# Attention and feed-forward on one core: the first product of seven tiles as Strassen's seven block products

## The chip, the core and the metric

The kernel runs on one core of a Trainium2 chip. Time is device microseconds (us) of one execution; lower is better. The core has TensorE (PE in the profile, its weight loads PEld), VectorE (DVE), ScalarE (ACT), GpSimd (POOL) and SyncE (SP), which only issues DMAs here. Each engine works through its own list in order; semaphores tie the lists together. A matmul takes a stationary operand of 128 columns (loaded first, `lhsT`) and streams a moving operand past it into PSUM.

## The reference

```python
# q, k, v: (8, 8, 576, 64) float32; w_in (512, 2048), w_out (2048, 512)
q_s = exp(q - max(q, -1));  q_s /= sum(q_s, -1) + 1e-9       # softmax over a row of 64
k_s = exp(k - max(k, 2));   k_s /= sum(k_s, 2) + 1e-9        # softmax over the sequence
kv  = einsum('bhsd,bhse->bhde', k_s, v)
att = einsum('bhsd,bhde->bhse', q_s, kv)
x   = att.transpose(0, 2, 1, 3).reshape(4608, 512)
h   = maximum(x @ w_in, 0)
out = (h * h) @ w_out
```

Nearly all the arithmetic is in the two products with `w_in` and `w_out`, both with 4608 rows of x.

## The kernel before

**Tiles.** The 4608 rows are nine tiles t = 0 to 8 of M = 512 columns (x is held transposed, features on the partitions). Tiles 0 to 7 are the first 512 rows of each batch, tile 8 the 64 last rows of all eight. While the feed-forward part works on tile t, the attention part makes tile t + 1, in four steps p of two heads each.

**Precision.** Each operand of a large product is split in a high part, rounded to float32r, and a low part, the rest: `split_x` makes xh on ScalarE and xl on VectorE, the weights are split once (`split_words`) into wi_h, wi_l, wo_h, wo_l, which stay in SBUF. A product is three matmuls: high by high, high by low, low by high.

**One tile.** For f = 0 to 15 (128 columns of w_in each), `first` makes a block h of 128 by 512 in a PSUM bank: 4 blocks of 128 features, 3 matmuls each, 12 of 512 columns. ScalarE makes r = relu(h), VectorE h = max(h, 0) * r, ScalarE gh = r squared and VectorE gl = h - gh (`split_g`). `second` adds gh and gl by w_out into four PSUM banks acc_0 to acc_3, again 12 matmuls of 512 columns, two groups later (LA = 2). The last two groups of `second` and the stores stand at the tile's end.

**Attention beside it.** For batches from 2 on q lies in blocks of 32; the maxima and sums of two half rows are exchanged by four small DMAs each (`swap_halves`, tiles sw_m and sw_s). `blocks_exp`, `blocks_norm`, `blocks_turn`, `blocks_split` make ql and qh; `k_max`, `k_shift_pool`, `k_exp` the keys; `kv_product` and `x_product` are its matmuls. `step`, `step_between` and `step_after` place these parts among the groups f, so a tile of the loop is written out in one order, and each engine's list is that order. Only tile 0 and what is before it is ordered by a planner.

## Time and profile before

| | |
|---|---|
| median of 3 runs | 883.64 us (883.05 to 884.48) |
| span of the profiled execution | 881.9 us |
| busy, PE / DVE / ACT / POOL | 865.1 / 485.8 / 359.7 / 186.8 us |
| tile 2 (232.62 to 326.29) | 93.67 us, PE busy 93.67 |
| tile 7, with no attention beside it (702.92 to 789.96) | 87.04 us |
| granted clock of TensorE | 0.998 of full |

The span is counted from the first to the last instruction of one profiled execution; the median is of unprofiled runs and is 1.7 us more. A matmul's shown duration (0.39 us for 512 columns) is longer than the step from one to the next, since matmuls overlap; the step is what counts. In the views a row gives line, engine, operation, output and inputs, count, busy time and mean of one in ns, and then the idle time ahead of it and what ended it. Nearly all instructions carry one line number, that of the helper which records them, so rows are told apart by tile names.

### The profile page before, as it was taken

How to read it: one execution, taken by the hardware profiler on the slowest of the kernel's cores; microseconds unless marked ns; L12 is line 12 of the kernel's file. 1: busy time of each engine (PE TensorE's matmuls, PEld its weight loads, DVE VectorE, ACT ScalarE, POOL GpSimd, SP SyncE). 2: the span in 40 equal slices, each digit the busy share in tenths (PEclk: the TensorE clock that was granted, in tenths of full speed). 3: DMA queues.
4: the chain of work that ended last, by engine and by line, in shares of the span. 5: the costliest groups of instructions: out<-in, count | busy, mean ns of one | idle time of the engine just before them, and what ended most of it. 6: DMA issues, size and time to landing. Idle time of an engine off the chain costs nothing.

```text
span 881.9 us, 12457 instructions
## 1 busy us (share of the span) xinstructions
PE 865.1 (98%) x4456; PEld 714.6 (81%) x4456; DVE 485.8 (55%) x897; ACT 359.7 (41%) x668; POOL 186.8 (21%) x237
## 2 busy tenths in 40 slices
PE   7899999999999999999999999999999999999997
PEld 6678888888888888788888888888888888888886
DVE  6888976554655465545654565556564532233222
ACT  5878854333434342335333343334233422232221
POOL 5789982111111101110111112110111000000000
PEclk9999999999999999999999999999999999999999
DMA  9992122211311122112311222113111110010002
GB/s 262 376 349 70 37 50 73 53 29 37 85 39 39 39 63 80 39 38 57 86 39 39 46 72 48 30 38 93 39 38 39 54 50 1 0 48 1 1 1 48
DMA packets 140878, 57.89 MB, mean 66 GB/s; under 512 B 115600, under 2 KB 134032, under 8 KB 140688
## 3 DMA queue, kind: packets, MB, share of 16 engines
q1 hardware_dynamic: 139104, 55.79, 23.6%
q10 hardware_dynamic: 1712, 1.31, 0.5%
q8 instruction: 35, 0.57, 0.3%
q14 instruction: 27, 0.22, 0.1%
HBM read 46.14 MB, written 10.49 MB: 64 GB/s over the span
## 4 chain that ended last, share of the span: by engine, by line
PE 91%; DMA 3%; DVE 3%; issue 1%; ACT 1%; SPq 1%; POOL 0%; DVEq 0%; POOLq 0%; ACTq 0%
PE acc L100 43%; PE h L100 42%; PE x L100 3%; PE kv L100 2%; DMA q<-in_q_dram 1%; DMA raw<-in_moe_w_in_dram 1%; DMA sw_m<-bmx 1%; SPq L100 1%; DVE km L100 1%; DMA kt<-in_k_dram 0%; DVE w L100 0%; POOL w L100 0%; DVE gl L100 0%; DVE up L100 0%; DVE qt L100 0%
## 5 line engine op out<-in xcount | busy, mean ns | idle before, releaser
L100 PE MATMUL h<-xh,w 128*128 128x512 f32 x1152 | 379.3, 392 | 3.2 <-DVE gl L100 3.1
L100 PE MATMUL acc<-w,gh 128*128 128x512 f32 x1152 | 355.7, 390 | 0.0
L100 PEld LDWEIGHTS h<-xh,w 128*128 128x128 f32 x1152 | 216.2, 188 | 50.3 <-DVE gl L100 4.4
L100 PEld LDWEIGHTS acc<-w,gh 128*128 128x128 f32 x1152 | 214.7, 188 | 43.4
L100 PE MATMUL h<-xl,w 128*128 128x512 f32 x576 | 224.3, 389 | 0.0
L100 PE MATMUL acc<-w,gl 128*128 128x512 f32 x576 | 224.2, 389 | 0.0
L100 DVE SCALAR_TENSOR_TENSOR h<-h,r 128x512 f32<-128x512 f32 x144 | 99.4, 691 | 101.8 <-ACT r L100 101.0
L100 DVE TENSOR_TENSOR gl<-h,gh 128x512 fp32r<-128x512 f32 x144 | 99.2, 689 | 92.2 <-ACT gh L100 83.7
L100 ACT ACTIVATE r<-h 128x512 f32<-128x512 f32 x144 | 85.1, 591 | 152.2 <-PE h L100 151.8
L100 ACT ACTIVATE gh<-r 128x512 fp32r<-128x512 f32 x144 | 90.7, 630 | 122.2 <-PE acc L100 113.7
L100 PEld LDWEIGHTS acc<-w,gl 128*128 128x128 f32 x576 | 108.1, 188 | 22.8
L100 PEld LDWEIGHTS h<-xl,w 128*128 128x128 f32 x576 | 108.2, 188 | 21.3
L100 POOL TENSOR_TENSOR k<-k,kmx 128x512 f32<-128x512 f32 x24 | 30.8, 1282 | 171.9 <-issue 143.1
L100 POOL PARTITION_ALL_REDUCE kmx<-km x24 | 17.4, 724 | 207.4 <-DVE km L100 166.2
L100 ACT ACTIVATE q<-q 128x576 f32<-128x576 f32 (+1 forms) x32 | 21.5, 672 | 96.7 <-DVE q L100 87.9
L100 POOL TENSOR_TENSOR w<-w,raw 128x512 int32<-128x512 int32 x32 | 42.0, 1320 | 7.9 <-DVE w L100 2.8
L100 POOL TENSOR_TENSOR w<-w,w 128x512 fp32r<-128x512 f32 x32 | 41.1, 1299 | 5.8 <-ACT w L100 5.7
L100 DVE SCALAR_TENSOR_TENSOR bsm<-bsm,sw_s 128x18 f32<-128x18 f32 x24 | 5.6, 232 | 61.4 <-DMA sw_s<-bsm 61.4
L100 ACT ACTIVATE raw<-raw 128x1024 f32<-128x1024 f32 (+1 forms) x32 | 36.3, 1148 | 2.2 <-DMA raw<-in_moe_w_in_dram 2.0
L100 DVE TENSOR_TENSOR bmx<-bmx,sw_m 128x18 f32<-128x18 f32 x24 | 4.2, 176 | 53.0 <-DMA sw_m<-bmx 53.0
L100 ACT ACTIVATE kvh<-kv,ks 64x64 fp32r<-64x64 f32 x64 | 19.8, 309 | 29.4 <-DVE ks L100 28.9
L100 ACT CAST qh<-qT 128x576 fp32r<-128x576 f32 (+1 forms) x32 | 20.9, 653 | 26.2 <-DVE qT L100 24.6
(104 smaller groups left out, 666.8 us busy)
## 6 DMA issues: line engine op xcount, KB each, us to landing
k<-in_k_dram SPq DMA_DIRECT2D x32, 256.0 KB, 2.7
raw<-in_moe_w_in_dram SPq DMA_DIRECT2D x16, 512.0 KB, 8.5
raw<-in_moe_w_out_dram SPq DMA_DIRECT2D x16, 512.0 KB, 8.8
out_dram<-o SPq DMA_DIRECT2D x32, 256.0 KB, 2.4
v<-in_v_dram SPq DMA_DIRECT2D x56, 128.0 KB, 2.9
q<-in_q_dram SPq DMA_DIRECT2D x96, 72.0 KB, 2.4
sw_m<-bmx SPq DMA_DIRECT2D x96, 2.2 KB, 1.7
sw_s<-bsm SPq DMA_DIRECT2D x96, 2.2 KB, 1.7
```

Of the source, the lines that this page charges most:

```text
L100: getattr(self.eng, op)(*map(real, args), **{k: real(a) for k, a in kwargs.items()})
```

## The change

Tiles 2 to 8 of the loop make the first product differently. Take two neighbouring groups of w_in columns, one = 2i and two = 2i + 1: 512 features by 256 columns, as 2 by 2 blocks of 256 by 128 (a11, a12 of group one, a21, a22 of group two), and x's tile as blocks b11, b12, b21, b22 of 256 features by 256 rows. Strassen's scheme in Winograd's form makes the four result blocks from seven block products instead of eight, with sums of blocks:

- of weights: s1 = a21 + a22, s2 = s1 - a11, s3 = a11 - a21, s4 = a12 - s2;
- of x: t1 = b12 - b11, t2 = b22 - t1, t3 = t2 - b11, t4 = b21 - t2.

Each of the seven operand pairs is again split in high and low, so a product is 2 x 3 matmuls of 256 columns (`product`). a11 b11, s2 t2, s3 t3 and a22 t4 add up one after the other in the left half of one PSUM bank (hu); ScalarE copies the running sum out after each (u1, u2, u3, c2's left half). s1 t1 and later s4 b22 add up in the right half of the other bank (hv), a12 b21 stands in its left. VectorE adds the pieces into c1 and c2 in SBUF and makes max(c, 0) * c; the high part is a copy on ScalarE, the low part of c2 is VectorE's, that of c1 GpSimd's.

The weights' sums don't fit in SBUF. In tile 1 they are made on GpSimd (`add_sums`), split (`split_sums`) and written to a DRAM buffer w_sums by ScalarE's queue (`keep_sums`), one of eight pairs at each of eight groups f; a11, a12 and a22 go there by SyncE (`begin_sums`). From tile 2 on, ScalarE's queue loads the pieces of pair n + 2 back into two rings of four former w_in slabs (`load_sums`), 1.8 MB per pair. The former slabs 2, 3 and 8 to 11 hold the split x parts. Tile 1's last two groups of `second` are carried over into tile 2; from then on `second` runs in eight units per pair, placed between the block products of the next pair, and the attention parts run two groups earlier (SKEW = 2), by new step functions.

On TensorE a pair of groups of tile 4 read like this before (group f = 5, the end of its first product and the start of a second):

```order
L100 MATMUL h_5_4501<-xh_2_4248,w_845 128x512
L100 MATMUL h_5_4501<-xh_3_4252,w_845 128x512
L100 MATMUL h_5_4501<-xl_3_4254,w_845 128x512
L100 MATMUL h_5_4501<-xh_3_4252,w_845 128x512
L100 MATMUL acc_0_4389<-w_845,gh_3_4441 128x512 x2
L100 MATMUL acc_0_4389<-w_845,gl_3_4443 128x512
L100 MATMUL acc_1_4393<-w_845,gh_3_4441 128x512 x2
L100 MATMUL acc_1_4393<-w_845,gl_3_4443 128x512
```

and now (pair f = 2, 3 of tile 5; h_3 is hu, h_2 is hv, each x6 row is one block product, the w names are slabs):

```order
L1138 MATMUL h_3_6122<-w_625,w_1342 128x256 x6
L1138 MATMUL h_2_6131<-w_709,w_1342 128x256 x6
L100 MATMUL acc_0_6138<-w_709,gh_1_6086 128x512 x2
L100 MATMUL acc_0_6138<-w_709,gl_1_6088 128x512
L1138 MATMUL h_3_6122<-w_1074,w_1420 128x256 x6
L1138 MATMUL h_2_6131<-w_1156,w_1420 128x256 x6
L100 MATMUL acc_1_6168<-w_709,gh_1_6086 128x512 x2
L100 MATMUL acc_1_6168<-w_709,gl_1_6088 128x512
L100 MATMUL acc_2_6172<-w_709,gh_1_6086 128x512 x2
L100 MATMUL acc_2_6172<-w_709,gl_1_6088 128x512
L1138 MATMUL h_3_6122<-w_1222,w_1486 128x256 x6
```

The second product, which stood in one piece of 12 matmuls behind a group, now stands in units of three between products that add into one PSUM block.

On ScalarE the end of a tile read like this before (x tile split, two stores, the next tile's first r and gh):

```order
L100 COPY xt_5504<-x_3_1_5941 128x64
L100 CAST xh_0_5948<-x_5497 128x512
L100 CAST xh_1_5952<-x_5497 128x512
L100 CAST xh_2_5956<-x_5497 128x512
L100 CAST xh_3_5960<-x_5497 128x512
L100 COPY o_0_5987<-acc_1_5247 128x512
L100 COPY o_2_6001<-acc_3_5255 128x512
L100 ACTIVATE r_0_6025<-h_0_6012 128x512
L100 ACTIVATE gh_0_6028<-r_0_6025 128x512
```

and now (end of the eighth pair of tile 4 and start of tile 5; ek and the 64x128 row are k's exponents, the w and b22xh casts the x parts t3, t4 and b22, kept is u1 and u2):

```order
L100 COPY c_15_5927<-h_15_5860 128x256
L100 DMA w_1486<-w_sums_107 128x1024
L100 CAST gh_15_5957<-c_15_5927 128x512
L100 CAST gh_14_5961<-c_14_5900 128x512
L100 DMA w_1566<-w_sums_107 128x512
L100 ACTIVATE ek_0_5969<-k_0_5665 128x2x4x64
L100 ACTIVATE spare<-spare 64x128
L100 CAST w_1222<-x_5248 128x512
L100 CAST w_1281<-x_5248 128x512
L100 CAST b22xh_5_5978<-x_5248 128x512
L100 COPY kept_0_5995<-h_1_5988 128x256 x2
```

The first copy out of hu of the new tile stands behind k's exponents and three casts of x parts. The core of the diff:

```diff
-    def second(f, parts, acc, c):
+    def second(f, parts, acc, c, begin=0, end=NF - 1):
         gh, gl = parts
         cs = slice(c * P, (c + 1) * P)
         with plan.together(True):
             for n, (a, w) in enumerate(((gh, wo_h), (gh, wo_l), (gl, wo_h))):
                 T.matmul(
                     out=acc[c], lhsT=a[:, cs], rhs=w[f],
-                    start=(f == 0 and n == 0), stop=(f == NF - 1 and n == 2),
+                    start=(f == begin and n == 0), stop=(f == end and n == 2),
+                )
+    def begin_sums(j):
+        one, two = slabs[2 * j], slabs[2 * j + 1]
+        for q, (slab, cols) in enumerate(
+            ((one, slice(0, HM)), (one, slice(HM, M)), (two, slice(HM, M)))
+        ):
+            Y.dma_start(
+                out=w_sums[j][:, 4 * q + 2:4 * q + 4, :], in_=slab[:, :, cols].bitcast(F32)
+            )
+    def add_sums(j):
+        one, two = slabs[2 * j], slabs[2 * j + 1]
+        full = cvt.tile([P, 2, M], F32, tag="w", name=f"full_{j}")
+        for i, slab in enumerate((one, two)):
+            G.tensor_tensor(out=full[:, i, :], in0=slab[:, 0, :], in1=slab[:, 1, :], op=ALU.add)
+        (a11, a12), (a21, a22) = ((full[:, i, 0:HM], full[:, i, HM:M]) for i in range(2))
+        sums = cvt.tile([P, 4, HM], F32, tag="w", name=f"sums_{j}")
+        s1, s2, s3, s4 = (sums[:, n, :] for n in range(4))
+        G.tensor_tensor(out=s1, in0=a21, in1=a22, op=ALU.add)
+        G.tensor_tensor(out=s2, in0=s1, in1=a11, op=ALU.subtract)
+        G.tensor_tensor(out=s3, in0=a11, in1=a21, op=ALU.subtract)
+        G.tensor_tensor(out=s4, in0=a12, in1=s2, op=ALU.subtract)
+        made["sums", j] = sums.rearrange("p n c -> p (n c)")
+    def split_sums(j):
+        sums = made.pop(("sums", j))
+        hi, lo = (slabs[i + 8 * (j > 5)].rearrange("p t n -> p (t n)") for i in range(2))
+        S.copy(out=hi, in_=sums)
+        V.tensor_tensor(out=lo, in0=sums, in1=hi, op=ALU.subtract)
+        made["split", j] = hi, lo
+        keep_sums(j, 0)
+    def keep_sums(j, i):
+        part = made["split", j][i]
+        to = w_sums[j].rearrange("p (n t) c -> p n t c", t=4)[:, :, i, :]
+        S.dma_start(out=to, in_=part.rearrange("p (n c) -> p n c", n=4).bitcast(F32))
+    RING = ((4, 5, 6, 7), (12, 13, 14, 15))
+    NAMES = (("s1", "a11"), ("s2", "a12"), ("s3", "a22"), ("s4",))
+    def load_sums(n, q, queue=S):
+        if n >= (B + 1 - WT) * (NF // 2):
+            return
+        slab = slabs[RING[n % 2][q]].rearrange("p t n -> p (t n)")
+        size = 2 * HM * len(NAMES[q])
+        src = w_sums[n % (NF // 2)].rearrange("p n c -> p (n c)")
+        queue.dma_start(out=slab[:, 0:size].bitcast(F32), in_=src[:, 4 * q * HM:4 * q * HM + size])
+    def sums_of(n):
+        w = {}
+        for q, names in enumerate(NAMES):
+            slab = slabs[RING[n % 2][q]].rearrange("p t (i c) -> p (t i) c", c=HM)
+            for i, name in enumerate(names):
+                w[name] = slab[:, 2 * i, :], slab[:, 2 * i + 1, :]
+        return w
+    X_AT = {"b11": 2, "t1": 3, "t2": 8, "b21": 9, "t3": 10, "t4": 11}
...
+    def x_sum(src, t, name):
+        b11, b12, b21, b22 = (x_part(src, n) for n in ("b11", "b12", "b21", "b22"))
+        if name == "t1":
+            G.tensor_tensor(out=b12, in0=b12, in1=b11, op=ALU.subtract)
+            made["t1"] = b12
+        elif name == "t2":
+            t2 = ffn.tile([P, M], F32, tag="xh1", name=f"t2_{t}", bufs=1)
+            t2 = made["t2"] = t2.rearrange("p (k c) -> p k c", k=2)
+            G.tensor_tensor(out=t2, in0=b22, in1=b12, op=ALU.subtract)
+        elif name == "t3":
+            G.tensor_tensor(out=b11, in0=made["t2"], in1=b11, op=ALU.subtract)
+            made["t3"] = b11
+        else:
+            G.tensor_tensor(out=b21, in0=b21, in1=made["t2"], op=ALU.subtract)
+            made["t4"] = b21
...
+    def split_part(src, t, name, eng=V):
+        hi, lo = x_halves(name, t)
+        one = made.pop(name) if name in made and name != "t2" else (
+            made["t2"] if name == "t2" else x_part(src, name))
+        S.copy(out=hi, in_=one)
+        eng.tensor_tensor(out=lo, in0=one, in1=hi, op=ALU.subtract)
+        return hi, lo
+    def product(out, w, x, begin):
+        (wh, wl), (xh, xl) = w, x
+        for k in range(2):
+            for i, (a, m) in enumerate(((wh, xh), (wh, xl), (wl, xh))):
+                nc.tensor.matmul(
+                    out=out.real(), lhsT=a[:, k * P:(k + 1) * P].real(), rhs=m[:, k, :].real(),
+                    start=(begin and k == 0 and i == 0), stop=(k == 1 and i == 2),
+                    skip_group_check=True,
                 )
...
+    def sums_step(f):
+        for j in range(NF // 2):
+            if f == 2 + j * 7 // 4:
+                split_sums(j)
+        for j in range(NF // 2):
+            if f == (2 + (j - 1) * 7 // 4 if j else 0):
+                add_sums(j)
+    def x_begin(src, t):
+        x = {"b11": split_part(src, t, "b11")}
+        x_sum(src, t, "t1")
+        x["t1"] = split_part(src, t, "t1")
+        return x
+    def x_first(src, t, x):
+        x_sum(src, t, "t2")
+        for n in ("t2", "b21"):
+            x[n] = split_part(src, t, n)
+        for n in ("t3", "t4"):
+            x_sum(src, t, n)
+        for n in ("t3", "t4", "b22"):
+            x[n] = split_part(src, t, n)
+        return x
...
+                if f % 2 == 0:
+                    begin_sums(f // 2)
+                if f == NF - 3:
+                    x_2 = x_begin(x_next, b)
+                if 9 <= f < 13:
+                    load_sums(0, f - 9, Y)
+                elif f >= 13:
+                    load_sums(1, f - 13, Y)
...
+        else:
+            x = x_first(x_next, b, x_2)
+            k_max(b + 1, 0)
+            k_shift_pool(b + 1, 0)
...
+            if t == WT and i == 0:
+                unit(4)
+            product(hu[:, left], w["a11"], x["b11"], True)
+            S.copy(out=u1, in_=hu[:, left])
+            if i == NF // 2 - 2 and b <= B:
+                x_sum(x_next, b, "t1")
+            add("t2")
+            if n == 0:
+                load_sums(1, 3)
+            turn("b11")
+            add("t3")
+            product(hv[:, right], w["s1"], x["t1"], True)
+            unit(1)
+            product(hu[:, left], w["s2"], x["t2"], False)
+            S.copy(out=u2, in_=hu[:, left])
+            load_sums(n + 2, 0)
+            turn("t1")
+            product(hv[:, left], w["a12"], x["b21"], False)
+            V.tensor_tensor(out=c1[:, left], in0=hv[:, left], in1=u1, op=ALU.add)
+            even_step(b_s, s)
+            unit(1)
+            if t == WT and i == 0:
+                k_exp(b, 0)
+                load_kq(b, 1, "k")
+            even_after(b_s, s)
+            unit(1)
+            product(hu[:, left], w["s3"], x["t3"], False)
+            S.copy(out=u3, in_=hu[:, left])
+            load_sums(n + 2, 1)
+            V.tensor_tensor(out=c2[:, right], in0=hv[:, right], in1=u3, op=ALU.add)
+            turn("t2")
+            turn("b21")
+            add("t4")
+            unit(1)
+            odd_between(b_s, s + 1, x_next)
+            unit(1)
+            product(hu[:, left], w["a22"], x["t4"], False)
+            S.copy(out=c2[:, left], in_=hu[:, left])
+            load_sums(n + 2, 2)
+            V.scalar_tensor_tensor(out=c2, in0=c2, scalar=0.0, in1=c2, op0=ALU.max, op1=ALU.mult)
+            product(hv[:, right], w["s4"], x["b22"], False)
+            V.tensor_tensor(out=c1[:, right], in0=hv[:, right], in1=u2, op=ALU.add)
+            V.scalar_tensor_tensor(out=c1, in0=c1, scalar=0.0, in1=c1, op0=ALU.max, op1=ALU.mult)
+            for f, g, eng, tags in ((two, c2, V, ("xl1", "xh2")), (one, c1, G, ("gh", "gl"))):
+                gh, gl = (
+                    ffn.tile([P, M], F32R, tag=tag, name=f"{kind}_{t}_{f}", bufs=1 if f == two else None)
+                    for kind, tag in zip(("gh", "gl"), tags)
+                )
+                S.copy(out=gh, in_=g)
+                eng.tensor_tensor(out=gl, in0=g, in1=gh, op=ALU.subtract)
+                parts[f] = gh, gl
+            load_sums(n + 2, 3)
+            odd_step(b_s, s + 1)
+            unit(1)
+            odd_after(b_s, s + 1, x_next)
+            for name in ("t3", "t4", "b22"):
+                turn(name)
+            unit(2)
+            if acc is None:
+                acc = begin_acc(t)
+            units += [(t, f, parts[f], acc, c, 1, NF - 2) for f in (two, one) for c in range(C)]
+            if split:
+                x = x_b
+        if t == B:
+            end_tile(t, parts, acc, NF - 1, NF - 2)
+            units.clear()
```

The attention parts of tiles from 2 on (`even_step`, `even_after`, `odd_between`, `odd_step`, `odd_after`) hold the same calls as the old steps, k and q one step further ahead, and q and the keys' tails use a former weight slab (`spare`) in turn with their old buffers.

178 lines of the change are left out of this document (156 added, 22 removed).

## The prediction

> **What bounds the kernel now.** I read the chain of waits first, then each tile as a window, then the rows of TensorE around single waits.
>
> ```profile
> PE 91%; DMA 3%; DVE 3%; issue 1%; ACT 1%; SPq 1%; POOL 0%; DVEq 0%; POOLq 0%; ACTq 0%
> 578.57 2.72 PE h L100 x12
> 138.84:232.62 93.78, 93.78 (x490) 77.69 (x489) 53.89 (x101) 35.50 (x70) 13.60 (x19) 1.00 0.23 52
> 326.29:421.09 94.80, 93.97 (x489) 77.58 (x489) 52.97 (x101) 35.50 (x70) 12.97 (x19) 1.00 0.23 52
> 421.09:515.38 94.29, 94.01 (x489) 77.58 (x489) 53.01 (x101) 35.29 (x70) 12.97 (x19) 1.00 0.23 52
> 515.38:609.09 93.71, 93.71 (x489) 77.65 (x489) 53.71 (x101) 35.40 (x70) 13.44 (x19) 1.00 0.23 52
> 702.92:789.96 87.04, 87.04 (x386) 72.07 (x385) 25.87 (x38) 22.93 (x38) 0.00 (x0) 1.00 0.07 26
> PE h L100 <- DVE gl L100: 3.1, 3, 2.0
> ```
>
> The chain is 91% TensorE. In the windows (length, then busy time of TensorE, weight loads, VectorE, ScalarE and GpSimd, clock, DMA share) TensorE never rests in an ordinary tile and the clock is 1.00; only the two windows from 326 to 515 run over 93.71, by 1.09 and 0.58 us, 1.7 in all. A tile without attention takes 87.04 us, so attention costs TensorE 6.7 us a tile. VectorE is busy 54 of 94 us, ScalarE 35. So time goes down only with TensorE's work, and up only if a queue beside it becomes late.
>
> **What the change takes off TensorE.** Twelve matmuls of 512 columns take 2.72 us: 0.2267 each. The nearest row to 256 columns is the 288-column product of attention:
>
> ```profile
> 599.67 0.29 PE L100 MATMUL x<-qh,kvh 128*128 128x288 f32 x1
> 599.80 0.19 PEld L100 LDWEIGHTS x<-ql,kvh 128*128 128x128 f32 x1
> 599.93 0.29 PE L100 MATMUL x<-ql,kvh 128*128 128x288 f32 x1
> 600.34 0.29 PE L100 MATMUL x<-ql,kvh 128*128 128x288 f32 x1
> ```
>
> Five steps from 599.67 to 600.34 are 0.134 each. The slope to 512 columns, (0.2267-0.134)/224 = 0.00041, gives 0.1207 for 256; I take 0.120. A pair of 128-column groups now costs 24 x 0.2267 = 5.44 us and then 42 x 0.120 = 5.04: 0.40 less, over 7 tiles x 8 pairs 22.4 us. The other bound is 0.134: that a weight load, not the columns, sets the step of 0.134. It would lose: 42 x 0.134 = 5.63, 0.19 more per pair. Against it speaks that 512 columns at 0.2267 and 288 at 0.134 lie on a line with nearly the same constant; I keep it as a rival.
>
> The Trainium skill, TensorE: Matmul & The Clock Gate, Back-to-back issue gap, has a warm step of N/2.4 ns + 2.5, and LDWEIGHTS there 128/1.2 = 107 ns, which would just hide. By it 256 columns take 0.109 and 512 take 0.216 (an estimate from that page). The trace disagrees at 512 by 0.011, with 0.2267.
>
> **What it adds to the other queues.** Per pair, ScalarE gives up two r and keeps two gh; it gains four copies of 256 columns out of PSUM and four DMA issues. VectorE trades two products and two subtractions for three adds of 256, two products and one subtraction; GpSimd takes the other subtraction. Prices:
>
> ```profile
> L100 ACT ACTIVATE gh<-r 128x512 fp32r<-128x512 f32 x144 | 90.7, 630 | 122.2 <-PE acc L100 113.7 <-issue 4.7 <-DVE qT L100 1.9
> L100 ACT CAST xh<-x 128x512 fp32r<-128x512 f32 x32 | 17.5, 622 | 0.0
> L100 ACT ACTIVATE ek<-k 128x512 f32<-128x512 f32 x28 | 17.6, 629 | 30.5 <-POOL k L100 30.3 <-DVE k L100 0.2
> L100 ACT ACTIVATE kt<-kt 64x128 f32<-64x128 f32 x28 | 8.5, 303 | 1.3 <-POOL kt L100 0.9
> L100 DVE TENSOR_TENSOR gl<-h,gh 128x512 fp32r<-128x512 f32 x144 | 99.2, 689 | 92.2 <-ACT gh L100 83.7 <-PE x L100 4.6
> L100 DVE TENSOR_TENSOR qtl<-qTt,qth 128x256 fp32r<-128x256 f32 x2 | 0.8, 409 | 0.0
> L100 POOL TENSOR_TENSOR k<-k,kmx 128x512 f32<-128x512 f32 x24 | 30.8, 1282 | 171.9 <-issue 143.1 <-DMA sw_s<-bsm 28.7
> 877.50 0.37 ACT L100 COPY o<-acc 128x256 f32<-128x256 f32 x1 [2.59 <-DVE o L100]
> 304.15 0.69 ACT L100 ACTIVATE q<-q 128x576 f32<-128x576 f32 x1 [5.02 <-DVE q L100]
> 304.74 0.62 ACT L100 ACTIVATE gh<-r 128x512 fp32r<-128x512 f32 x1
> 354.31 0.50 PE L100 MATMUL h<-xh,w 128*128 128x512 f32 x1 [0.83 <-DVE gl L100]
> ```
>
> So 0.37 for a copy of 256 columns (I use 0.38), 0.42 for a VectorE add of 256 (qtl 0.409), 1.28 on GpSimd; instructions in a row start some 0.08 before the one ahead ends (304.15 + 0.69 against 304.74), and a TensorE that stood still loses about 0.11 more on its first matmul (0.50 for 0.39).
>
> The DMA issue on ScalarE has no row beside compute. SyncE's and the two extreme rows:
>
> ```profile
> 704.00 0.40 SPq L100 DMA_DIRECT2D x<-x_tail  x1
> L100 SPq DMA_DIRECT2D raw<-in_moe_w_out_dram x16: 431/909/2832, 16.7 to 58.6; - x16
> ```
>
> One issue of long rows takes 0.40, behind a full queue 0.91. It stands right behind a copy of 0.38 that ScalarE executes meanwhile. Bounds: 0 if it runs wholly beside the copy, 0.91 if it is serial behind a full queue. I take 0.1, since 0.40 beside 0.38 leaves little; the queue is not full: 1.8 MB per pair of 10.5 us is 170 GB/s, while the page's second and third slices moved 376 and 349.
>
> ```profile
> GB/s 262 376 349 70 37 50 73 53 29 37 85 39 39 39 63 80 39 38 57 86 39 39 46 72 48 30 38 93 39 38 39 54 50 1 0 48 1 1 1 48
> ```
>
> **Where TensorE will wait.** The four products on one PSUM block (a11, s2, s3, a22) are running sums: each is copied out before the next may add. Between a11 and s2 lie s1 and one unit of the second product, 0.72 + 0.68 = 1.40 us; a copy that starts 0.2 after a product and takes 0.38 fits, unless ScalarE's queue is behind. I walked the four queues through one tile by these durations; they are behind at four places.
>
> (a) Tile ends. Counted from the end of a22 in the eighth pair, VectorE still has two low halves of x parts (0.69 each), c2's product, the add and c1's product: 3 x 0.61 + 0.46 + 0.69, from 0.1 before, so ScalarE's second gh starts at 2.9. Behind it: gh 0.52, issue 0.1, k's exponent 0.55, kt 0.22, three casts 3 x 0.54, the copy u1 0.42: u1 is there at 6.33. TensorE wants it after s4 0.72, three units 2.04, a11, s1 and a unit 2.12: 4.88. It waits 1.45 + 0.11 = 1.6, entering tiles 3 to 6: 6.4. Entering 7 and 8 no k stands there: 0.5 each. Entering 2, GpSimd's three sums in a row (3 x 1.28) delay the casts: 1.0.
>
> (b) Second pair: two stores of the previous tile and qh stand before u1: 0.5 in five tiles, 2.5.
>
> (c) Pairs with attention's products (third and seventh): ql on VectorE ends 0.14 after its x product is due, and xt, which waits for VectorE's km, holds u1 by 0.24: 0.76 a tile, 3.8 in five tiles.
>
> (d) a22 of the eighth pair waits for u3 behind attention's exponent: 0.2, four times, 0.8.
>
> In the second tile GpSimd adds per pair two sums of 512 and four of 256, 2 x 1.28 + 4 x 0.7 (half of 1.28 and a little) = 5.4 us, 43 in a tile where it had 13.6; ScalarE a copy of 1024 and two issues, VectorE a subtraction of 1024. What they delay is gl, needed two groups later, which leaves some 3 us; they cost nothing as long as a sum is ready within one group (5.4 us) and I put 1.0 for where it isn't. SyncE issues 24 writes and seven loads more there, 31 x 0.40 = 12 us among attention's swaps; a load waits for the sums that read its slab, and swaps stand behind it, with two groups of room.
>
> **Sum.** 16.5 us of new waits (8.4 + 2.5 + 3.8 + 0.8 + 1.0), minus 22.4 and minus the 1.7 that the two long windows lose today: -7.6. The span of 881.9 becomes 874.3; the median 883.64 lies 1.74 above the span, so **876.0 us**. With issues at 0.40, (a) is 2.1, (b) 0.8, (d) 0.5: about 881. With 0 about 875.
>
> **Rivals.**
>
> *The waits do not come:* if ScalarE and VectorE have more slack than my walk gives (c stays), the time is 883.6 - 24.1 + 3.5 = 863. For it: ScalarE is busy only 35 of 94 us now. Against: it works in order, and the waits are of queue order, not load.
>
> *The weight load sets the step (slower):* 42 matmuls of 256 columns step at 0.134, as the 288-column ones. 56 x 0.19 = 10.6 more, with the waits halved, since TensorE is later: 883.6 + 10.6 - 1.7 + 8 = 900. It decides from 0.1295 per matmul (5.44/42), where the product gains nothing. For it:
>
> ```profile
> L100 PEld LDWEIGHTS x<-qh,kvl 128*128 128x128 f32 x64 | 12.0, 188 | 1.2
> L100 PEld LDWEIGHTS kv<-v,ek 128*64 128x64 f32 x512 | 17.6, 137 | 6.5 <-issue 5.8 <-ACT ek L100 0.7
> ```
>
> A load of 128 columns shows 0.188, and starts only when the matmul ahead starts (599.80). Against: 64 more columns cost 0.051, so 128 occupy about 0.10.
>
> *ScalarE's issues are dear (slower):* at 0.91 each and serial, a pair gives ScalarE 3.6 us more; (a) becomes 3.1, (b) 1.3, (d) 1.0 and every second pair's s2 waits 0.3: waits near 36, time 883.6 - 24.1 + 36 = 895. It decides from about 0.5 an issue, where gain and waits cancel. The swaps of attention's maxima share the DMA engines with the new loads and would add to it:
>
> ```profile
> L100 SPq DMA_DIRECT2D sw_m<-bmx x96: 569/588/892, 139.0 to 677.6; - x96
> DMA to landing us min/median/max: 1.7/1.7/3.3
> ```
>
> Four issues of 0.59 and 1.7 to landing, 4.1 us, have 7 us of room in my walk.
>
> *A shorter step:* the rows at 288 and 512 columns share a constant, 0.134 - 288 x 0.00041 = 0.015. Were it not paid at 256, the step would be 0.106: 56 x 42 x 0.014 = 33 more off TensorE, and by my walk a third of it back as waits: 854. Against it: both rows pay it. The rule of the Trainium skill quoted above is of this kind.
>
> **Chances.** My forecast 0.48, no waits 0.18, weight load 0.12, dear issues 0.17, a shorter step 0.05. Around the forecast 868 to 884. A measurement here tells 0.2%, 1.8 us: faster is below 881.9. Of my own 0.48, 0.36 lie there, 0.07 within, 0.05 above 885.4. Faster 0.36 + 0.18 + 0.05 = 0.59, same 0.07, slower 0.05 + 0.12 + 0.17 = 0.34. Range 861 to 896, from no waits to dear issues.
>
> **What would show it.** Six matmuls of one product start 0.72 us apart end to end (0.80 for the weight-load rival); TensorE's waits name ScalarE's u1 (`kept`) at tile ends, 1 to 2 us; few waits inside pairs four, five and six; an attention tile falls only from 93.7 to about 93.5, the last two from 87.0 to about 84.4; the second tile stays near 93.8. I am wrong if s2 or s3 waits in every pair, if c1's low half on GpSimd comes late for the second product, or if loads land too late for their pair.

## The result, and the profile after

The changed kernel takes **1108.7 us** (median of 3 runs, 1103.5 to 1110.4) against 883.6: a ratio of 1.254 with an interval of 1.249 to 1.258. The profiled execution, the slowest of the three, spans 1108.6 us, 226.7 more than before.

The page of the changed kernel gives, for each engine, its busy time and instructions, then the granted clock of TensorE in 40 slices and the engines' shares of the chain of waits:

```profile
span 1108.6 us, 15448 instructions
PE 918.7 (83%) x5464; PEld 787.8 (71%) x5464; DVE 550.1 (50%) x1038; ACT 393.1 (35%) x809; POOL 340.2 (31%) x369
PEclk9999999998798979989789997898988889999999
PE 44%; issue 14%; DMA 14%; DVE 13%; ACT 7%; POOL 6%; SPq 1%; ACTq 0%; DVEq 0%; POOLq 0%
```

TensorE was 91% of the chain and is now 44%; it stands still for 190 us. Even its busy time is 54 us longer, though its columns are fewer: the granted clock is below 0.9 in 14 of the 40 slices. Three windows of the changed kernel, from the first copy u3 of a tile to that of the next (length, busy time of the engines in the order of the page, clock, DMA share, GB/s): tiles 3 and 4 with attention beside them, tile 7 without:

```profile
417.60:551.20 133.60, 104.07 (x633) 89.90 (x633) 60.73 (x119) 38.91 (x89) 28.84 (x30) 0.89 0.51 147
551.20:684.00 132.80, 103.77 (x633) 89.32 (x633) 60.73 (x119) 38.90 (x89) 28.30 (x30) 0.88 0.52 148
934.10:1019.60 85.50, 84.64 (x530) 76.15 (x529) 34.51 (x57) 26.50 (x57) 15.50 (x12) 1.00 0.60 197
```

So the product itself does what it was meant to: without attention a tile takes 85.50 us instead of 87.04. With attention it takes 133 instead of 94, and the second tile loses too: the first copy u3 of the loop starts at 287.5, while the old tiles would put it near 236 (an estimate: the groups of tile 1 end at 227.2, 232.62 less its last eight units of 0.68, and seven units and five block products of 0.72 stand ahead of u3). The waits of the changed kernel, with their total, number and longest:

```profile
POOL gl L100 <- ACT gh L100: 330.9, 38, 11.8
POOL k L100 <- issue: 166.0, 21, 9.6
ACT ek L100 <- POOL k L100: 112.2, 19, 12.2
PE h L1138 <- ACT kept L100: 82.7, 30, 6.7
PE h L1138 <- ACT c L100: 32.6, 4, 8.4
```

TensorE waits for u1 (`kept`, the name of u1 and u2), as the prediction said, but for 82.7 us: u1 stands in ScalarE's list behind the keys' exponent ek, ek waits for the keys k from GpSimd, and k waits for "issue". What that is, the timeline of the changed kernel shows (start, duration, engine, then in brackets the idle time ahead and what ended it; the second row completes km, the maxima of each row):

```profile
487.08 1.30 POOL L100 TENSOR_TENSOR gl<-c,gh 128x512 fp32r<-128x512 f32 x1 [11.18 <-ACT gh L100]
487.99 0.54 DVE L100 TENSOR_TENSOR km<-km,spare 64x128 f32<-64x128 f32 x1
494.34 0.72 POOL L100 PARTITION_ALL_REDUCE kmx<-km  x1 [5.96 <-DVE bmx L100]
503.01 1.25 POOL L100 TENSOR_TENSOR k<-k,kmx 128x512 f32<-128x512 f32 x1 [7.95 <-issue]
504.30 0.63 ACT L100 ACTIVATE ek<-k 128x512 f32<-128x512 f32 x1 [4.03 <-POOL k L100]
505.28 0.37 ACT L100 COPY kept<-h 128x256 f32<-128x256 f32 x1
505.71 2.93 PE L1138 MATMUL h<-w,w 128*128 128x256 f32 x12 [3.29 <-ACT kept L100]
```

The all-reduce of the keys' maxima (km to kmx) is shown with 0.72 us, but GpSimd does nothing else from 488.38 to 503.01: **14.6 us**, 5.96 ahead of the shown row and 7.95 behind it. Hardly any of that is a wait for km, which was complete at 488.53. In the kernel before the idle time is nearly as long, but km was late in it:

```profile
439.65 0.28 DVE L100 TENSOR_TENSOR km<-km,kt 64x128 f32<-64x128 f32 x1
442.30 0.72 POOL L100 PARTITION_ALL_REDUCE kmx<-km  x1 [5.89 <-DVE h L100]
449.71 1.28 POOL L100 TENSOR_TENSOR k<-k,kmx 128x512 f32<-128x512 f32 x1 [6.69 <-DMA sw_s<-bsm]
```

From the beginning of that idle time, 436.41, to 449.71 are 13.3 us, of which 3.5 had gone when km was complete (439.93). So the first part ran beside the wait for km, and the keys came 9.8 us after km; over all 24 all-reduces of the kernel before it was 7.6 to 10.9. In the changed kernel, from the sixth all-reduce on, it is 13.3 to 16.2: c1's low part (gl) stands directly ahead on GpSimd and ends some 0.15 us before km, so the first part no longer runs beside the wait for km but behind it. The all-reduce is asked for at the end of a pair (`odd_step`), and the exponent of its keys stands at the end of the next (`k_exp`), one pair of 10.5 us later.

The rows close into a ring. From one k to the next, 472.73 to 503.01, go 15.65 us for k, ek, u1, a pair and its c1 (to the end of gl at 488.38) and 14.63 us for the all-reduce, 30.3 in all. At the change of tile the same all-reduce holds TensorE by another way: x's sum t2 stands behind it on GpSimd, ScalarE's cast of t2 waits for that, and c2's copy out of hu stands behind the cast (`c`, some 8 us in each of four tiles).

### The profile page after: what moved, and what is told of

Read it like the earlier page. It is cut to its first block, busy times and chain, and to the rows that moved or that the text cites. A ratio compares the mean times of both kernels' runs of the same rounds, so it can differ in the third digit from the quotient of the medians.

```text
span 1108.6 us, 15448 instructions
## 1 busy us (share of the span) xinstructions
PE 918.7 (83%) x5464; PEld 787.8 (71%) x5464; DVE 550.1 (50%) x1038; ACT 393.1 (35%) x809; POOL 340.2 (31%) x369
## 4 chain that ended last, share of the span: by engine, by line
PE 44%; issue 14%; DMA 14%; DVE 13%; ACT 7%; POOL 6%; SPq 1%; ACTq 0%; DVEq 0%; POOLq 0%
PE acc L100 19%; PE h L1138 17%; PE h L100 5%; DMA spare<-in_q_dram 4%; DVE c L100 3%; DMA sw_m<-bmx 3%; POOL k L100 3%; PE kv L100 2%; DMA w<-w_sums 2%; DVE km L100 2%; ACT w L100 1%; DMA w_sums<-w 1%; SPq L100 1%; DVE qT L100 1%; ACT ek L100 1%
## 5 line engine op out<-in xcount | busy, mean ns | idle before, releaser
L1138 PE MATMUL h<-w,w 128*128 128x256 f32 x2016 | 310.3, 303 | 145.5 <-ACT kept L100 82.7
L1138 PEld LDWEIGHTS h<-w,w 128*128 128x128 f32 x2016 | 293.1, 208 | 183.2 <-ACT kept L100 97.8
L100 POOL TENSOR_TENSOR gl<-c,gh 128x512 fp32r<-128x512 f32 x56 | 72.2, 1290 | 357.7 <-ACT gh L100 330.9
L100 DVE TENSOR_TENSOR c<-h,kept 128x256 f32<-128x256 f32 x112 | 47.0, 420 | 229.2 <-PE h L1138 220.5
L100 PE MATMUL h<-xh,w 128*128 128x512 f32 x256 | 90.2, 413 | 18.0 <-DVE gl L100 18.0
L100 DVE SCALAR_TENSOR_TENSOR c<-c 128x512 f32<-128x512 f32 x112 | 81.9, 731 | 41.6 <-ACT c L100 39.7
L100 ACT CAST gh<-c 128x512 fp32r<-128x512 f32 x112 | 69.6, 622 | 80.6 <-DVE c L100 79.9
L100 PEld LDWEIGHTS h<-xh,w 128*128 128x128 f32 x256 | 50.2, 196 | 32.0 <-DVE gl L100 21.2
L100 ACT ACTIVATE ek<-k 128x512 f32<-128x512 f32 x28 | 17.6, 628 | 114.2 <-POOL k L100 112.2
L1138 PE MATMUL h<-b22xh,w 128*128 128x256 f32 x224 | 52.1, 295 | 0.0
L100 PE MATMUL h<-xl,w 128*128 128x512 f32 x128 | 51.6, 403 | 0.0
```

The lines of the kernel that those rows point to most:

```text
L100: getattr(self.eng, op)(*map(real, args), **{k: real(a) for k, a in kwargs.items()})
L1138: nc.tensor.matmul(out=out.real(), lhsT=a[:, k * P:(k + 1) * P].real(), rhs=m[:, k, :].real(), start=(begin and k == 0 and i == 0), stop=( ...
```

## The experiments

Six groups of runs, each beside the kernel before on the same chip (medians 883.0 to 884.4). "u3 at" is the start of the loop's first copy u3, which tells how late the second tile and the change to the third are.

**Without the all-reduce.** In the change, and as a control in the kernel before, a GpSimd copy of km stands for it, so the maximum across rows is left out:

```
-        G.partition_all_reduce(kmx, km, channels=P, reduce_op=RED.max)
+        G.tensor_copy(out=kmx, in_=km, n=128)
```

> The changed kernel with GpSimd's maximum across partitions (partition_all_reduce of km) replaced by a plain copy of km on GpSimd; so the keys are shifted by each row's own maximum and that part of the computation is left out. Theory A (the all-reduce holds GpSimd some 14 us, k's exponents wait for it in ScalarE's list, and the copies out of PSUM wait behind them): the steps of two pairs fall from 30.5 us to 22 to 23.5 and the time to 875 to 895. Rival B (ScalarE's order as such, with its copies and DMA issues, or the 170 GB/s of weight loads): the time stays above 1050.

> The kernel before with the same all-reduce replaced by the same plain copy (the same part left out). Theory A: there the all-reduce has two groups of time to spare and is hidden, so 883 as before, within 2 us; GpSimd's gap before k's subtraction vanishes. If the before kernel gained more than 5 us as well, the all-reduce would not be what the change made visible.

Measured: 945.8 us in the change (ratio 1.070, 1.067 to 1.072), 882.5 in the kernel before (0.998, 0.996 to 1.000). The all-reduce costs 163 us here, and was hidden before. The page of the change without it:

```profile
span 942.0 us, 15352 instructions
PE 875.1 (93%) x5464; PEld 752.6 (80%) x5464; DVE 555.5 (59%) x1038; ACT 393.1 (42%) x809; POOL 332.6 (35%) x369
```

The same 5464 matmuls are busy 43.6 us less: that much of the 163 was TensorE working slower after its waits (its clock, in the last section), the rest the waits. But 62 us remain above the kernel before, so the expectation of 875 to 895 missed: there is more than one cause.

**The same maximum by TensorE and VectorE**, as the first batches make it: a transpose of km, a row maximum, a diagonal of it and a product with ones, and VectorE subtracts.

```
-            k_shift_pool(*ahead(b, p, 1))
+        # at the next pair: k_turn_max(b, p) in even_step, k_shift_pe(b, p) in odd_between
```

> The changed kernel with the keys' maximum across rows made as the second batch has it already: km turned by TensorE, reduced by VectorE, spread by a product with ones, k shifted by VectorE. GpSimd keeps only c1's low parts, ql and the x sums. Theory A: 875 to 900, with the second tile near 95 us. Rival B: above 1050.

Measured: 949.6 us (1.073, 1.070 to 1.076). The gain is as large, and the expected 875 to 900 missed again: it is the all-reduce on GpSimd that costs, not the maximum.

**Only c1's low part away from GpSimd** (to VectorE), the all-reduce kept:

```
-            for ... in ((two, c2, V, ("xl1", "xh2")), (one, c1, G, ("gh", "gl"))):
+            for ... in ((two, c2, V, ("xl1", "xh2")), (one, c1, V, ("gh", "gl"))):
```

> The changed kernel with the low part of c1 made by VectorE instead of GpSimd; GpSimd keeps the all-reduce. Theory A: the chain all-reduce, k's subtraction, k's exponent, first copy out of PSUM is untouched, 1050 to 1110. Rival C (what TensorE waits for is c1's low part behind the all-reduce in GpSimd's list): below 950.

Measured: 1002.5 us, one run, between the theory's 1050 and the rival's 950: both missed. The loss falls by 106 us. The trace of this run shows that the edit does two things:

```profile
349.39 0.29 DVE L100 TENSOR_TENSOR km<-km,kt 64x128 f32<-64x128 f32 x1
349.82 0.73 POOL L100 PARTITION_ALL_REDUCE kmx<-km  x1 [12.41 <-DMA w<-w_sums]
357.97 1.76 POOL L100 TENSOR_TENSOR k<-k,kmx 128x512 f32<-128x512 f32 x1 [7.43 <-PE h L1138]
```

No low part of the second product stands behind the all-reduce any more, and none stands directly ahead of it: GpSimd is free 12 us before km is complete, the shown all-reduce starts 0.14 us behind km, and k 8.3 us behind it, where it was 14.5. How much of the 106 us each of the two is worth, this run can't tell.

**The all-reduce asked for half a pair earlier**, c1's low part on VectorE:

```
     def even_after(b, s):        # i == 2
+            k_max(*ahead(b, p, 1)); k_shift_pool(*ahead(b, p, 1))
     def odd_step(b, s):          # i == 3
-            k_max(*ahead(b, p, 1)); k_shift_pool(*ahead(b, p, 1))
```

> The change with GpSimd's all-reduce of the keys' maxima issued half a pair earlier (behind the adds of the second pair's first half instead of at its end), and c1's low part on VectorE, so that nothing of the second product stands behind the all-reduce; the result is the full one. Theory A (the all-reduce occupies GpSimd some 14 us and is only asked for too late): from its new place it has about 17 us until the keys' exponent is due, so it is hidden and the time falls to what the change has without the all-reduce, 940 to 960 us. Rival (GpSimd is simply too full: 14.3 for the all-reduce, 1.3 for the subtraction and 1.5 for a low part of q in every 22 us, in whichever order): the keys still come late, 985 to 1005.

Measured: 985.7 us (1.114, 1.110 to 1.117), the rival's number. But the trace places it elsewhere than the rival did: of the 43 us that this run is longer than the one without the all-reduce, 23 lie ahead of the first u3, most of it in the second tile. A window of this run over that tile:

```profile
137.20:258.00 120.80, 93.54 (x447) 73.90 (x446) 60.90 (x101) 39.26 (x69) 60.26 (x67) 0.91 0.56 172
```

GpSimd shows 60.3 us there, four all-reduces among them with 0.7 each; at some 14 each they make 114 of 120.8 us. That gave the next run, with the all-reduce replaced **in the second tile only** (and for the first keys of the tile after it):

```
     def prepare(b, p): k_max(b, p)
-        k_shift_pool(b, p)
     def step / step_after:       # tile 1
+        k_turn_max(b, p)  ...  k_shift_pe(b, p)
```

> The change with the all-reduce asked for half a pair earlier and c1's low part on VectorE (985.7 us), and only the keys whose maxima are made during the second tile by TensorE and VectorE instead of the all-reduce. Theory G (in the second tile GpSimd is overfull: four all-reduces of 14.3 us, 43 us of sums and some 7 us of other work in a tile that had 94 us, and everything from there on starts 22 us late): 960 to 968 us, with the first copy u3 of the loop near 265 instead of 286. Rival (the early all-reduce loses its time evenly in all tiles): 978 to 986.

Measured: 967.7 us (1.093, 1.089 to 1.098), as theory G had it, at the end of its range. The start of the first copy u3, with the all-reduce in the second tile and without, 21.3 us apart:

```profile
286.36 0.35 ACT L100 COPY last<-h 128x256 f32<-128x256 f32 x1
```

```profile
265.07 0.35 ACT L100 COPY last<-h 128x256 f32<-128x256 f32 x1
```

From there on the early all-reduce costs little: by the starts of u3, tiles 3 to 5 take 104.3 to 107.1 us in the first of the two runs, against 99.8 to 102.3 without any all-reduce and 131 to 134 in the change. But the earlier place did the smaller part of that: with the all-reduce where the change has it and only c1's low part on VectorE, the same tiles take 108.6 to 109.8. So in the loop it was mainly c1's low part on GpSimd beside the all-reduce that cost, and in the second tile GpSimd's load.

**SyncE's order.** From here on the base is the version with the maximum by TensorE and VectorE (949.6 us). Its SyncE queue, VectorE's wait, ScalarE and TensorE around one copy u3:

```profile
419.47 0.71 DVE L100 TENSOR_REDUCE bmx<-q 128x18 f32<-128x576 f32 x1
419.58 2.29 SPq L100 DMA_DIRECT2D spare<-in_q_dram  x4
421.98 4.74 SPq L100 DMA_DIRECT2D sw_m<-bmx  x4
429.81 0.18 DVE L100 TENSOR_TENSOR bmx<-bmx,sw_m 128x18 f32<-128x18 f32 x1 [2.70 <-DMA sw_m<-bmx]
430.81 0.68 ACT L100 ACTIVATE q<-q 128x576 f32<-128x576 f32 x1 [3.27 <-DVE q L100]
431.40 0.35 ACT L100 COPY last<-h 128x256 f32<-128x256 f32 x1
431.81 0.97 PE L1138 MATMUL h<-w,w 128*128 128x256 f32 x6 [1.61 <-ACT last L100]
```

The maxima are there at 420.18, but the loads of the next queries stand first, then the four swaps take 4.74 us to issue and the last lands at 429.8; q's exponent and u3 follow. The edit:

```
+            blocks_max(*ahead(b, p, 1))
             load_q(*ahead(b, p, 2))
-            blocks_max(*ahead(b, p, 1))
```

> The change with the keys' maximum made across rows by TensorE and VectorE (949.6 us), and in SyncE's queue the four swaps of the query maxima issued ahead of the four loads of the next queries, not behind them. Theory S (SyncE's order: the loads' issues take 2.3 to 6.4 us, the swaps wait behind them, and ScalarE's exponent of q, which waits for the swaps, stands ahead of the copy that TensorE waits for): the waits for the copy before s4 and a22 fall from 2 to 4 us each to under 1, tiles 2 to 5 of the loop from about 103.6 to 97 to 99 each, 922 to 934 us in all. Rival D (the swaps are slow because the weight loads share the DMA engines: a swap lands after 2.9 us where it took 1.7): the order matters little, 944 to 950.

Measured: 933.9 us (1.057, 1.054 to 1.060), 15.7 less; at the slow end of theory S (of tiles 2 to 5, two took the 97 to 99 us that it gave, the others 99.7 and 101.6). The same place now, in the run with the swaps first:

```profile
415.89 0.71 DVE L100 TENSOR_REDUCE bmx<-q 128x18 f32<-128x576 f32 x1
416.63 2.47 SPq L100 DMA_DIRECT2D sw_m<-bmx  x4
419.14 2.64 SPq L100 DMA_DIRECT2D spare<-in_q_dram  x4
423.44 0.17 DVE L100 TENSOR_TENSOR bmx<-bmx,sw_m 128x18 f32<-128x18 f32 x1
```

VectorE uses the swaps 6.8 us after the maxima's end instead of 9.6, waits for nothing, and TensorE's wait for u3 in tile 3 is 0.23 us. A tile with attention (tile 3), before and after this edit:

```profile
369.30:471.90 102.60, 96.95 (x645) 84.13 (x645) 65.06 (x131) 40.24 (x94) 18.61 (x18) 0.98 0.67 191
```

```profile
366.70:464.90 98.20, 94.36 (x646) 82.79 (x645) 64.92 (x131) 40.23 (x94) 18.64 (x18) 1.00 0.69 200
```

It is still 4.5 us above the 93.7 of the kernel before. Of the 3.8 us that TensorE waits in it, 3.1 are for u1 behind row ends of ScalarE's list, the kind and size that the prediction had.

**The second tile.** With the swaps first, 50.5 us of span remain above the kernel before. By the starts of u3 they are: 29 up to the first u3 (265 for 236), 23 in tiles 2 to 5, 1.4 in tile 6, less 3 in tiles 7 and 8. The next runs go after the 29. First, two groups for each sum of weights instead of one or two, on the 949.6-us base:

```
-            if f == 2 + j * 7 // 4: split_sums(j)
+            if f == min(2 * j + 2, NF - 1): split_sums(j)
-            if f == (2 + (j - 1) * 7 // 4 if j else 0): add_sums(j)
+            if f == 2 * j: add_sums(j)
```

> The change with the keys' maximum by TensorE and VectorE (949.6 us), and in the second tile every sum of weights gets two groups between its additions on GpSimd and its split on ScalarE (seven of eight; the steps were one or two groups). Theory T (a sum takes GpSimd 6 to 7 us and more with a low part of q ahead of it, so after one group ScalarE stands at the split and all of the tile's own work behind it): the waits of 6.2, 3.5 and 1.7 us in the second tile go, 932 to 940 us. Rival (the tile is lost to the amount of work, VectorE's low parts of 1024 columns and ScalarE's copies of 1024, wherever they stand): 945 to 950.

Measured: 948.2 us (1.072, 1.067 to 1.077): nothing, the rival's number. TensorE's wait of 6.3 us early in the tile fell to 0.5, but one of 3.5 at its end became 3.9, and at the change to the next tile TensorE stood 6.17 us for u1, where it had stood 1.16:

```profile
258.73 2.93 PE L1138 MATMUL h<-w,w 128*128 128x256 f32 x12 [6.17 <-ACT kept L100]
```

Ahead of u1 in ScalarE's list stood the casts of x's t3 and t4, which wait for GpSimd. Both edits together with q's exponent put behind u3:

```
     even_step, i == 0:      - blocks_exp(b, p)
     odd_between, i == 1:    + blocks_exp(b, p)
```

> The last two edits together, and the exponent of q on ScalarE behind the copy that TensorE waits for (u3) instead of ahead of it. Theory: the edits add up, and the exponent, however late its swaps are, no longer holds TensorE: tiles 2 to 5 of the loop at 94 to 97 us, second tile near 95 to 100, 900 to 918 us in all. Rival (the second tile and the small waits that show once the large ones are gone take it back): 920 to 935.

Measured: 951.3 us (1.077, 1.073 to 1.081), a miss: 17 more than with the swaps alone. With the exponent behind u3 the waits moved to u1 and to VectorE's adds (in tile 3, 4.9 us for u1 and 1.3 for c); this edit was dropped. Then the casts of t3, t4 and b22 behind u1 and u2:

```
     x_first:                - for n in ("t3", "t4", "b22"): x[n] = split_part(src, t, n)
     tile 2, behind u1:      + x["t3"] = split_part(x_now, t, "t3")
     tile 2, behind u2:      + x["t4"], x["b22"] likewise
```

> The version with the keys' maximum by TensorE and VectorE and the swaps ahead of the query loads (933.9 us), with two groups for every sum of weights but the last, and with the splits of x's t3, t4 and b22 at the change of tile taken out of the row ahead of the first product's copies u1 and u2 and put behind them. Theory X (in the run with the even sums ScalarE's casts of t3 and t4, which wait for GpSimd, stood ahead of u1, and TensorE waited 6.2 us there: what the second tile gained was lost at its end): with the casts behind the copies both gains are kept, the first pair's copy u3 comes 9 to 14 us earlier (265 becomes 251 to 256) and the time is 918 to 926 us. Rival (the chain of x's sums on GpSimd itself, t2 to t4 with casts between, is late by the same amount): 930 to 936.

> The same three edits on the change with GpSimd's all-reduce replaced by a plain copy of one row's maxima (the maximum across rows is left out; 945.8 us without the edits). Theory: with no all-reduce on GpSimd and no transposes on TensorE for it, only the waits in the order of ScalarE, SyncE and GpSimd are left; an attention tile takes 94 to 97 us, 908 to 918 us in all, so the change would still lose 25 to 35 us with a free maximum. Rival (TensorE's transposes and VectorE's shifts in the other version hold back more than the trace shows): 890 to 905.

Measured: 931.6 us (1.054, 1.051 to 1.057), u3 at 265.6: theory X fell, and the number is its rival's; the wait only took another name. The same edits with the maximum across rows left out: 921.8 us (1.042, 1.038 to 1.045), u3 at 258.6. So the maximum on TensorE and VectorE costs 9.9 us, 7.0 of them ahead of the first u3, and even with a free maximum the change stays 38 us above the kernel before, a little over what was expected.

In that 931.6-us version the four swaps of a late pair of the second tile took 4.18 us to issue, and VectorE stood 7.88 for them:

```profile
216.64 4.18 SPq L100 DMA_DIRECT2D sw_m<-bmx  x4
223.95 0.18 DVE L100 TENSOR_TENSOR bmx<-bmx,sw_m 128x18 f32<-128x18 f32 x1 [7.88 <-DMA sw_m<-bmx]
228.58 0.79 PE L100 MATMUL h<-xh,w 128*128 128x512 f32 x1 [5.27 <-DVE gl L100]
```

So all transfers of sums in that tile went to ScalarE's queue:

```
-            Y.dma_start(out=w_sums[j]...          load_sums(0, f - 9, Y)  load_sums(1, f - 13, Y)
+            S.dma_start(out=w_sums[j]...          load_sums(0, f - 9)     load_sums(1, f - 13)
```

> The last full version (keys' maximum by TensorE and VectorE, swaps first, two groups per sum, casts behind the copies; 931.6 us), and in the second tile all 24 writes of w_in blocks and all seven first loads of sums issued from ScalarE's queue instead of SyncE's, so that SyncE's queue there carries attention's small transfers only. Theory Q (in that tile four swaps of the query maxima behind a 512 KB load took 4.2 us to issue and landed 8.7 after the maxima, and VectorE and ScalarE stood for them in order, TensorE 5.3 behind these): the swaps land in 4 to 5 us, the second tile loses 6 to 12 us less, the first copy u3 comes near 255 instead of 265.6 and the time is 918 to 926 us. Rival (the swaps share the 16 DMA engines with the same bytes from any queue; 264 GB/s there): they still land late, 929 to 934.

Measured: 938.7 us (1.064, 1.061 to 1.067), u3 at 270.4: slower, and outside both expected ranges. The swaps did come sooner (four issued in about 2.5 us each time, 3.6 at most to landing where it was 6.7), but now ScalarE stood in its own issues:

```profile
213.61 3.57 ACTq L100 DMA_DIRECT2D w_sums<-w  x4
217.22 0.52 ACTq L100 DMA_DIRECT2D w<-w_sums  x1
217.79 0.60 ACT L100 ACTIVATE r<-h 128x512 f32<-128x512 f32 x1 [5.35 <-DMA w_sums<-w]
```

Last, three runs that leave out work of the second tile, on the 931.6-us version. In the first one copy stands for GpSimd's six additions per sum, so the sums are left out; in the second the split is cut to 8 of 1024 columns, so the split is left out; in the third both:

```
-        full = ...; G.tensor_tensor(...) x6
+        G.tensor_copy(out=sums, in_=one)
-        S.copy(out=hi, in_=sums); V.tensor_tensor(out=lo, in0=sums, in1=hi, op=ALU.subtract)
+        the same on [:, 0:8]
```

> The full version with swaps first, even sums and casts behind the copies (931.6 us; its first copy u3 of the loop at 265.6, some 29 later than tiles before it would allow), with GpSimd's six additions per sum of weights left out: one copy of 1024 columns stands for them, so the sums are not the reference's. Theory P (GpSimd's additions, 5.5 to 8 us a sum, are what the second tile waits for): u3 at 246 to 254, 912 to 921 us. Rival (with two groups for each sum GpSimd no longer decides; the splits on ScalarE and VectorE or the transfers do): u3 at 260 or later, 926 to 932.

> The same version with the additions kept, and the split of the sums (ScalarE's copy of 1024 columns, 1.05 us, and VectorE's subtraction of 1024, 1.2 to 1.6 us, eight of each) cut to 8 columns, so that the split is left out. Theory V (VectorE and ScalarE in order: 2.3 to 2.7 us a sum ahead of the tile's own low parts, 20 in all): u3 at 248 to 256, 914 to 922 us. Rival (the splits have room beside the tile's own work): u3 at 261 or later, 927 to 932.

> Both cuts together; what stays in the second tile are the 16 writes of sums, the 24 writes of blocks and the seven loads. Theory C (compute work decides): u3 at 240 to 246, 905 to 913 us. Rival M (the transfers decide: attention's swaps and loads share 16 DMA engines that are 60 to 90% busy there): u3 at 255 or later, 921 to 930.

Measured: 930.8 (1.053, 1.047 to 1.059), 927.3 (1.050, 1.047 to 1.054) and 926.9 us (1.049, 1.045 to 1.052), with u3 at 260.3, 258.0 and 256.8. The first copy u3 without either:

```profile
256.81 0.37 ACT L100 COPY last<-h 128x256 f32<-128x256 f32 x1 [1.01 <-PE h L1130]
```

Theories P, V and C missed. The first run met its rival's numbers, the second its rival's time though not its u3, and the third met rival M's, the transfers. All the compute work that the second tile got explains 9 of the 29 us of u3 (5.3 by the additions alone, 7.6 by the split alone), and tiles 2 to 5 took 4 of these back. Where the other 20 come from is not shown. Candidates are the transfers (207 GB/s there, where it was 60), the change of tile, whose chain of x sums stayed in all runs, and the maximum on TensorE and VectorE, whose absence moved u3 by 7.0 above. In the last run TensorE's waits of over 0.4 us from 137 to u3 are 12.8 us: 4.6 ahead of attention's x products, 3.6 for gl, 2.8 for the maximum, 1.8 for u1. Why tiles 2 to 5 took 4 us back stays open too. No version beat the kernel before.

## Why the prediction was wrong

876.0 us in 861 to 896 was predicted, 1108.7 came. Point by point:

**The gain: right.** Twelve matmuls of 256 columns of the changed kernel take 1.59 us, the last of them 0.28:

```profile
500.13 1.59 PE L1138 MATMUL h<-w,w 128*128 128x256 f32 x12
```

(1.59 - 0.28) / 11 = 0.119 against 0.120. The rival of the weight load (0.134, 900 us) and that of a shorter step (0.106, 854) are both out. Pairs without attention follow each other after 10.5 us, as the prediction's 5.04 and 5.44 add up to; tile 7 took 85.5 where it said 84.4, since the pair at the tile's change takes 11.7.

**"GpSimd takes the other subtraction": here the prediction failed.** The walk through the four queues has no term for GpSimd's list. In (a) it lets k's exponent follow gh and the issue with 0.55 us, as if the keys were there, so ScalarE's wait for k stands at nothing; measured, it is 112.2 us in 19 waits, and TensorE's wait for u1 behind it 82.7. The busy 13.6 us that the prediction gives GpSimd for a tile count each all-reduce with its shown 0.72, though the row that the prediction itself quoted for k has 143.1 us of "issue" idle time over 24 subtractions, 6 us each. With 14.6 for the all-reduce, GpSimd's work for a step of two pairs is 14.6, 1.3 for k, 0.5 for the tail, 1.4 for ql and twice 1.3 for c1's low part, 20.4 us. That would just go into two pairs of 10.5, but not in the ring shown above, where the pair and the all-reduce follow one another: the steps last 30.3 us, from one wait for u1 to the next:

```profile
475.42 2.93 PE L1138 MATMUL h<-w,w 128*128 128x256 f32 x12 [5.34 <-ACT kept L100]
505.71 2.93 PE L1138 MATMUL h<-w,w 128*128 128x256 f32 x12 [3.29 <-ACT kept L100]
```

That is 160 of the 226.7 us (span 1108.6 against 948.3 with the maximum elsewhere): 23 up to the first u3, 113 in tiles 2 to 5 and 24 in tile 6. "I am wrong if ... c1's low half on GpSimd comes late for the second product" is what happened; that it comes late because of the all-reduce, and makes the next all-reduce late in turn, was not seen.

**"Four issues of 0.59 and 1.7 to landing, 4.1 us, have 7 us of room": wrong in the size.** In the rows shown they took 9.6 us from the maxima. The order of SyncE's queue is worth 15.7 us; with the swaps first they take 6.8 at most, since VectorE no longer waits for them.

**The second tile, +1.0: wrong by an order.** "43 us in a tile where it had 13.6" was right for GpSimd's additions (a sum takes 2.55 and four times 0.73, 5.5), but the four all-reduces of the same tile were again left out, which costs 21 us; 29 more are lost without them. The sums don't "cost nothing": without their splits u3 comes 7.6 us earlier, without their additions 5.3. But the runs give all this compute work together only 9 of the 29; the rest of that term stays open.

**The waits at tile ends and in pairs, 8.4 + 2.5 + 3.8 + 0.8: right in kind, once the rest is mended.** With the maximum off GpSimd and the swaps first, TensorE waits 7.4 us in tile 2, 3.8 in each of tiles 3 to 5, 1.9 and 0.9 in the next two, 15.1 of it for u1 and u2: 21.6 us, where the prediction had 15.5.

**ScalarE's issues, 0.1 each: right for the loop, nearer to the bound of 0.** An issue takes 0.33 us there and runs beside the copy of 0.37 ahead of it:

```profile
482.04 0.37 ACT L100 COPY last<-h 128x256 f32<-128x256 f32 x1 [4.55 <-PE h L1138]
482.05 0.33 ACTq L100 DMA_DIRECT2D w<-w_sums  x1
```

The dear issue of the rival, 0.91 and serial, does exist: four writes in a row took 3.57 us when the second tile's transfers all stood in that queue. That rival's total of 895 has nothing to do with the result.

One reading was a little off and changes nothing: instructions in a row overlap by 0.10 us in the rows quoted for it (304.15 + 0.69 against 304.74), where the prediction says 0.08.

## What to carry to other kernels

An instruction's shown duration is not its cost to its queue: price a library operation such as an all-reduce by the time from the end of its engine's work ahead to the start of the work behind, 14 us for a shown 0.72 (only some 8 of them count where its input comes late in that time), and read "issue" idle time in a quoted row as part of it. When a change rewrites the order of a loop, list for each engine what it must do in one step, hidden work included, and for each hidden operation what stands directly ahead of it and how far its result's use now lies from its start: here an idle GpSimd had hidden the first 6 us of the all-reduce, and a low part put ahead of it brought them out. Small exchanges that stand behind loads in the same queue are late by the loads' issues, and so is everything in order behind them.

## What the runs showed of the hardware that was not expected

A wait of TensorE can cost more than its length. After 5.34 and after 3.29 us of standing still, twelve matmuls took 2.93 us instead of 1.59; the profile has the granted clock at 0.50 until 481.63 and 508.93. But the length of the wait alone doesn't decide it. Two waits for u1 of the same length, in the 931.6-us run:

```profile
362.93 1.70 PE L1138 MATMUL h<-w,w 128*128 128x256 f32 x12 [2.10 <-ACT kept L100]
559.34 2.93 PE L1138 MATMUL h<-w,w 128*128 128x256 f32 x12 [2.09 <-ACT kept L100]
```

And one of 2.45 us, in the change, behind which six matmuls took 0.98 instead of 0.88:

```profile
496.38 0.98 PE L1138 MATMUL h<-w,w 128*128 128x256 f32 x6 [2.45 <-ACT last L100]
```

In ten traces of this case, all changes of the granted clock, from 130 us on and but for the last 60, lie on a grid of 3.41 us. Cut along that grid, a window of full clock in which TensorE was busy for less than 45% was followed by one at 0.50 in 82 of 82 cases, one busy for 45 to 55% in 10 of 38, one busy for more in none of 2006. In the second of the rows above the wait lies in one window, which was busy for 40%; in the first it is shared by two, busy for 85 and 54%. In the change the clock is at 0.50 for 177 us, with TensorE busy in 123 of them; without the all-reduce for 27, busy in 26. At half speed half of that busy time is lost, 61 against 13 us (an estimate): enough for the 43.6 us of longer busy time.

The Trainium skill, TensorE: Matmul & The Clock Gate, Part 1 (The HAM clock gate), says that the clock falls to half after an idle window of about 3.4 us, and that the window runs free. The grid here agrees with a free-running window; that the window must be idle does not, since one that was busy for 40% was enough.

Which queue issues a transfer moves the waiting, not the load: taken off SyncE, the transfers let the swaps pass and held ScalarE for 5.35 us instead, and the time rose by 7 us. The Trainium skill, DMA: Bandwidth & Descriptors, Issuing engines are not separate DMA queues, has it that issuing from several engines saves only the issuing sequencer's time, usually small beside the transfer. Here too an issue of these writes took 0.54 us and the landing 4.0 (medians in that tile), but four in a row took 3.57 us of an engine that also computes.
